# Attention and SwiGLU on one core: first loads from two queues, and the order planned anew

## The chip, the core and the metric

The kernel runs on one core of a Trainium2 chip, as one program. A core has five engines that work beside each other and wait for each other through semaphores: TensorE (PE, matrix products), VectorE (DVE), ScalarE (ACT), GpSimd (POOL) and SyncE (SP, here used only to issue transfers). Transfers between the chip's memory and the core's are issued by an instruction on one engine's queue and carried out by 16 DMA engines. The metric is the device time of one launch in microseconds (us).

## The reference

A forgetting attention over 8 batches of 8 heads, 576 positions and 64 channels, and behind it a feed-forward block with SwiGLU over the 4608 tokens, whose inner width is 1536:

```python
scores = scale * np.matmul(q, k.transpose(0, 1, 3, 2))
cum = np.cumsum(np.log(np.clip(f, 0.0001, 1.0)), axis=-1)
scores = np.where(causal, -1e9, scores + cum[..., :, None] - cum[..., None, :])
attn = np.exp(scores - np.max(scores, axis=-1, keepdims=True))
attn = attn / (np.sum(attn, axis=-1, keepdims=True) + 1e-09)
x = np.matmul(attn, v)          # (8, 8, 576, 64), then (4608, 512)
g = x @ w_gate                  # (512, 1536)
out = (g / (1 + np.exp(-g)) * (x @ w_val)) @ w_out
```

All inputs and the output are float32; the kernel multiplies in bfloat16.

## The kernel before, in words

**Attention** runs over 32 pairs of heads (`p`, four to a batch). A pair's 576 query positions are nine blocks of 64, and the two heads of a pair lie in the two halves of the 128 partitions. Blocks 0 to 3 are part A (`g` = 0) and blocks 4 to 8 part B (`g` = 1). For each pair the steps are:

- loads of `q`, `k` and of the cumulated log gates `cb`, spread over the partitions; the first four pairs get them in parts (`load_parts`, L523), the others whole (`load_pair`, L453 and L460);
- casts to bfloat16 (`qb`, `kb`; L560 to L564, later L481 and L483), transposes on PE (L207) into `tx`, copies out of it into `qz` and `kt` (L589 and L591, later L509 and L511);
- scores on PE into `sp` (L201), with a mask added by a small matmul for the first half of the pairs; DVE adds `cb` and takes the row's minimum at once (L652, tiles `t` and `tm`); ACT takes the exponential and its row sum (L672, tiles `e`, `eo` and `ls`); DVE inverts the sums (`lr`, L688 and L690, or L686 on ACT first); POOL, or ACT for the first eight pairs, multiplies by them (`pk`, L708 or L706);
- `pk` is transposed: for the first eight pairs on PE through `gv` with a copy to `pT` (L743), then by a DMA transpose from SP (L721);
- `pT` times `vt` on PE (L764) and a copy into `xT` (L791), which holds a ring of 2048 tokens, transposed for the feed-forward block.

**The cumulated gates** are made once: `f` is loaded (L398), clipped by DVE (L400), its logarithm taken by ACT (L402), and summed along the positions by a DVE scan (L403). The first pairs get their rows of it by a float32 matmul with a selecting matrix (`select`, L425, copied out at L430); the others read them back from a buffer in the chip's memory (`cum_f`, L412).

**The feed-forward block** runs over twelve tiles of tokens (256, 256, seven of 512, 256, 128, 128). `gate` multiplies `xT` by pieces of `w_gate` and `w_val` (both L201, into `gv`, from `wg` and `wv`), with tanh on ACT (L855) and two products on DVE (L857, L860) into `hh`; `project` multiplies `hh` by `w_out` (`wo`), copies out (L884, L886) and stores (L889). The weights are loaded by POOL, which casts them on the way, in eleven pieces (L824 and L828): `wg2` is columns 256 to 511 of `w_gate`, named after its first block of 128 columns. The first tile of tokens needs part A of all four pairs of the first batch, and for its first group `wg0` and `wv0`, for its second `wg2` and `wv2`.

**What sets the order.** The program names every operation with the engines that could do it and an estimate of its duration on each, with a priority and its dependences. `Plan.order` then places the operations one by one: always the one that could start soonest on some engine (a `bias` can be added to an engine's start for the comparison), ties by priority. That gives each engine's order of instructions, and for operations with a choice also the engine. A buffer is given to its next user in order of priority; `SLACK` (`pl.slack`) says how long one group of users of a pool lets another go first. `NUDGE` shifts the priorities of named groups of operations: `a` a pair's attention part, `q` its preparation, `v` a batch's values, `f` and `o` a tile's gates and projection. No time is measured while the kernel runs; the order is fixed when it is built.

**The line of first loads.** `STARTUP` (L281) lists the first loads in order: `q1` is the last part of pair 1's `q`, `p0` part A of `k` and `q` of pairs 0 and 1 in two halves each (called `k0A` and `q0A` in the prediction), `p2` the same for pairs 2 and 3 (`k2A`, `q2A`), `k0` and `q0` the parts B, `f9` the gates, `c3` the `cb` rows of pair 3, `v04` the fifth block of batch 0's values, `wg2` a piece of weights. The loop at L930 gives them priorities in this order, ties each to the end of the load ten places before it (`AHEAD`), and a load of weights, which is POOL's, to the one six places before (`BEHIND`). These ties hold for the plan. Before the change ACT issues two of the first loads, one half of `k0A` and one of `q0A`, POOL the weights, and SP all others.

Of the kernel before, what the change touches and what calls it, by code (L numbers as in the profile page):

```python
# [214 lines left out]
def kernel(  # L215
# [11 lines left out]
    nc = tc.nc  # L227
# [36 lines left out]


    NHALF = 4
    NSELA = 4
    NSEL = 1
    CUT = QB * (HI[0] + 1)
# [2 lines left out]
    BEHIND = 6  # L272
# [12 lines left out]
    NUDGE = "a0.0:-91 a0.1:-64.5 a1.0:-94.5 a1.1:-57.5 a11.1:-0.5 a12.1:-0.5 a14.0:-1.5 a15.0:-2.5 a16.0:-4 a16.1:-1 a18.0:-0.5 a19.1:-1 a2.0:-83.5 a2.1:-46 a20.0:-0.5 a23.0:-1.5 a24.0:-2.5 a24.1:-1.5 a25.0:-1.5 a25.1:-3 a26.0:0.5 a26.1:-3.5 a28.0:4.5 a29.0:-1 a3.0:-78.5 a3.1:-57 a30.0:3.5 a30.1:0.5 a31.0:22 a31.1:8 a4.0:-42.5 a4.1:-28.5 a5.0:3 a5.1:-39.5 a6.0:-3.5 a6.1:3 a7.0:1.5 a7.1:-13 a8.0:1 a8.1:0.5 f0:-981.5 f11:18.5 f2:3 f4:4 f5:2 f6:-1.5 f8:1 f9:-4 o0:1.5 o1:-18.5 o10:-2 o3:0.5 o5:-5 o6:-1 o7:9.5 o8:-0.5 o9:5 q0:-42.5 q1:-75.5 q11:1 q12:2 q14:-0.5 q15:-0.5 q16:-3.5 q17:-0.5 q18:-6 q20:-5.5 q21:0.5 q22:1.5 q23:1 q24:3.5 q25:2 q28:3 q29:1 q3:1.5 q31:5.5 q5:-0.5 q6:0.5 q8:-1.5 q9:-3.5 v1:-57.5 v2:3.5 v3:5.5 v4:5.5 v5:5.5 v6:2 v7:-2.5"  # L285

    WAIT = ""
    ORDER = [(int(u[0]), int(u[1])) for u in HEAD.split()]
# [7 lines left out]
    pl = Plan()  # L296
# [98 lines left out]
    def gates(key, parts, np_, prio):  # L395
        x = lambda: pl.buf(key)[0:np_, :]
        for n, (a, z, src) in enumerate(parts):
            loads["f", key, n] = pl.op({"SP": 600}, lambda e, a=a, z=z, src=src: nc.sync.dma_start(out=pl.buf(key)[a:z, :], in_=src),  # L398
                                       (), [(key, 0)] + [key] * (n == 0), prio + n * .01, dma=570, pk=93)
        pl.op({"DVE": 760}, lambda e: nc.vector.tensor_scalar(x(), x(), 1.0e-4, 1.0, op0=ALU.max, op1=ALU.min),  # L400
              [(key, 0)], [(key, 1)], prio, holds=[key])
        pl.op({"ACT": 690}, lambda e: nc.scalar.activation(x(), x(), AF.Ln), [(key, 1)], [(key, 2)], prio, holds=[key])  # L402
        pl.op({"DVE": 1350}, lambda e: nc.vector.tensor_tensor_scan(x(), tiny[0:np_, 0:1].to_broadcast((np_, S)), x(), 0.0, ALU.mult, ALU.add),  # L403
              [(key, 2), "tiny"], [(key, 3)], prio, holds=[key])
# [118 lines left out]
    def load_parts(p):  # L523
        b, hp = divmod(p, NPB)
        pl.key(("cb", p), "cb", p)
        for name, x, a, z, r, n in parts(p):
            fk = (name + "f", p, x)
            pl.key(fk, name + "f")
            m = (z - a) // r

            def load(e, u, fk=fk, src=(k if name == "k" else q), a=a, z=z, r=r, m=m):
                h0 = 2 * (hp + u)
                (nc.scalar if e == "ACT" else nc.sync).dma_start(
                    out=pl.buf(fk)[m * u:m * u + m, :, 0:r * D],
                    in_=src[b, h0:h0 + 2, a:z].rearrange("h (p r) d -> p h (r d)", r=r))
# [262 lines left out]
    def load_v(b):  # L798
        for c in range(5):
# [107 lines left out]
    line = []  # L907
# [97 lines left out]
```

## Time and profile before

| | us |
|---|---|
| median of three runs | 413.37 |
| the three runs | 416.99, 413.37, 410.46 |
| the profiled execution | 410.55 |
| its span, first to last instruction | 408.8 |
| PE, busy | 391.2 |
| DVE, busy | 334.5 |
| ACT, busy | 319.8 |
| POOL, busy | 271.5 |

The three engines beside PE have no idle engine's worth of room either: DVE does the scores' sums and the gates' products, ACT the exponentials and tanh. The table's busy times are those of the whole span, but the span has three stages. Up to about 30 us only attention runs, as no tile of tokens is finished. From there to about 330 us attention and the feed-forward block run beside each other, and the rest is the feed-forward block alone. In a row of the timeline the columns are the start, the duration, the engine, line and operation, the tile written and the tiles read, shapes and types, how many instructions are merged, and in brackets the idle time just before with what ended it. In the rows of PE a duration includes the way through the array, so that durations of neighbours overlap.

### The profile page before, as it was taken

Reading aid. Unit: us, or ns where it says so; the run is one execution under the profiler, and the core shown is the slowest. Engines: PE = TensorE matmul, PEld = TensorE weight load, DVE = VectorE, ACT = ScalarE, POOL = GpSimd, SP = SyncE. Lnnn points to the kernel's source line nnn. Section 1 sums busy time; section 2 is a strip of 40 time slices with the busy share of each in tenths; the row PEclk is TensorE's granted clock in tenths of the full one; section 3 lists DMA queues with packets and bytes.
Section 4 is the critical chain, followed back from the end, with each engine's and each line's share of the span. In section 5 each row is a group of like instructions: output and inputs, shape, how many; then the busy total and the mean of one; then the engine's idle time right before and its main releaser. Section 6 shows DMA issues by size and latency. Waiting matters only on the chain.

```text
span 408.8 us, 15353 instructions
## 1 busy us (share of the span) xinstructions
PE 391.2 (96%) x5848; PEld 266.0 (65%) x5848; DVE 334.5 (82%) x1270; ACT 319.8 (78%) x905; POOL 271.5 (66%) x474
## 2 busy tenths in 40 slices
PE   2978899999999999999999999999999999999996
PEld 1657879887776776665655655565565555577766
DVE  4698999979998789989999998899989943775123
ACT  5898999999999989998978998897889753332222
POOL 8579877989888985898798797967957550000000
PEclk9999999999999999999999999999999999999999
DMA  7999997997999999999999999999975584000211
GB/s 203 239 211 188 230 195 142 188 251 203 193 216 176 248 231 202 225 253 226 208 204 234 219 228 216 238 193 208 220 175 110 107 135 130 2 2 2 102 57 53
DMA packets 144026, 72.16 MB, mean 177 GB/s; under 512 B 117904, under 2 KB 131728, under 8 KB 143952
## 3 DMA queue, kind: packets, MB, share of 16 engines
q1 hardware_dynamic: 137856, 66.21, 75.8%
q0 software_dynamic: 5808, 4.72, 7.9%
q8 instruction: 45, 0.74, 0.8%
q14 instruction: 29, 0.24, 0.2%
q10 hardware_dynamic: 288, 0.26, 0.2%
HBM read 46.65 MB, written 9.58 MB: 138 GB/s over the span
## 4 chain that ended last, share of the span: by engine, by line
PE 85%; ACT 3%; DVE 3%; DMA 3%; POOL 3%; issue 1%; POOLq 0%; DVEq 0%; ACTq 0%
PE gv L201 64%; PE sp L201 9%; PE tx L764 5%; PE tx L207 4%; DMA wv<-in_moe_w_val_dram 2%; PE gv L207 2%; DVE t L652 2%; PE gv L425 1%; DMA qf<-in_q_dram 1%; POOL pk L708 1%; ACT eo L672 1%; ACT e L672 1%; ACT pT L743 1%; DVE th L857 0%; ACT qz L589 0%
## 5 line engine op out<-in xcount | busy, mean ns | idle before, releaser
L652 DVE CUSTOM_DVE_ANT_0 t<-sp,cb 128x512 f32<-128x512 f32 (+7 forms) x272 | 121.3, 464 | 9.0 <-PE sp L201 5.4
L708 POOL TENSOR_SCALAR pk<-e,lr 128x128 bf16<-128x128 f32 (+3 forms) x188 | 100.2, 537 | 30.3 <-DVE lr L690 20.5
L201 PE MATMUL gv<-xT,wv 128*64 128x512 bf16 (+2 forms) x1152 | 112.5, 326 | 1.2 <-DMA wv<-in_moe_w_val_dram 1.2
L201 PE MATMUL gv<-xT,wg 128*64 128x512 bf16 (+2 forms) x1152 | 112.6, 326 | 0.0
L201 PE MATMUL gv<-wo,hh 128*64 128x512 bf16 (+1 forms) x888 | 106.1, 373 | 0.0
L857 DVE SCALAR_TENSOR_TENSOR th<-th,gv 128x512 f32<-128x512 f32 x108 | 73.9, 685 | 28.3 <-ACT th L855 26.9
L672 ACT ACTIVATE e<-t,tm 128x192 f32<-128x192 f32 (+4 forms) x160 | 88.9, 557 | 8.4 <-DVE tm L652 7.6
L855 ACT ACTIVATE th<-gv 128x512 f32<-128x512 f32 x108 | 64.0, 593 | 32.9 <-PE gv L201 32.1
L201 PE MATMUL sp<-kt,qz 128*64 128x64 bf16 (+7 forms) x640 | 76.6, 292 | 3.2 <-DVE tm L652 2.4
L860 DVE TENSOR_TENSOR hh<-th,gv 128x512 bf16<-128x512 f32 x108 | 73.8, 684 | 4.6 <-PE gv L201 1.8
L201 PEld LDWEIGHTS <-wg 128*64 128x64 bf16 x1152 | 59.0, 110 | 27.7
L201 PEld LDWEIGHTS <-wv 128*64 128x64 bf16 x1152 | 58.1, 110 | 28.2 <-DMA wv<-in_moe_w_val_dram 1.4
L672 ACT ACTIVATE eo<-t,tm 128x256 f32<-128x256 f32 (+3 forms) x128 | 71.2, 557 | 5.1 <-DVE tm L652 2.7
L708 POOL TENSOR_SCALAR pk<-eo,lr 128x384 bf16<-128x384 f32 (+2 forms) x127 | 67.7, 533 | 9.8 <-DVE lr L690 4.1
L201 PEld LDWEIGHTS <-hh 128*64 128x64 bf16 x888 | 48.9, 110 | 31.2
L201 PEld LDWEIGHTS <-qz 128*64 128x64 bf16 x640 | 41.0, 112 | 21.2 <-issue 4.8
L652 DVE DVE_READ_ACCUMULATOR2_ANT tm<- 128x1 f32 x432 | 35.8, 83 | 0.0
L884 ACT ACTIVATE ot<-gv 128x512 f32<-128x512 f32 (+1 forms) x31 | 18.0, 581 | 22.2 <-PE gv L201 21.9
L652 DVE CUSTOM_DVE_ANT_0 t<-sp,cm,tm 128x64 f32<-128x64 f32 x128 | 34.4, 278 | 0.9 <-PE sp L201 0.2
L672 ACT ACTIVATION_READ_ACCUMULATOR e<-t,tm 128x1 f32 x160 | 30.6, 191 | 0.0
L764 PE MATMUL tx<-pT,vt 128*64 128x320 bf16 (+4 forms) x448 | 29.2, 262 | 1.4 <-DVE pT L743 0.6
L481 POOL TENSOR_SCALAR qb<-qf 72x1024 bf16<-72x1024 f32 x28 | 29.1, 1040 | 1.2 <-DVE tm L652 0.7
(75 smaller groups left out, 436.1 us busy)
## 6 DMA issues: line engine op xcount, KB each, us to landing
out_dram<-ot SPq DMA_DIRECT2D x35, 256.0 KB
vf<-in_v_dram SPq DMA_DIRECT2D x32, 256.0 KB
cb<-cum_f SPq DMA_DIRECT2D x56, 144.0 KB
kf<-in_k_dram SPq DMA_DIRECT2D x28, 288.0 KB
qf<-in_q_dram SPq DMA_DIRECT2D x28, 288.0 KB
wo<-in_moe_w_out_dram POOLq DMA_DIRECT2D x3, 512.0 KB, 5.9
vf<-in_v_dram SPq DMA_DIRECT2D x8, 128.0 KB
wg<-in_moe_w_gate_dram POOLq DMA_DIRECT2D x2, 512.0 KB, 7.7
```

The source lines that it names most:

```text
L201: nc.tensor.matmul(out[c, :], lhsT[:, c], rhs, **kw)
L207: nc.tensor.transpose(out[c, :], src[:, c], ident)
L425: nc.tensor.matmul(pl.buf(bk)[:, 0:z - a], w, pl.buf("fa")[0:BH, a:z], start=True, stop=True)
L481: eng[e].tensor_scalar(dst, src, -scale, 1.0, op0=ALU.mult, op1=ALU.mult)
L652: nc.vector.tensor_tensor_reduce(out=pl.buf(tk)[:, a:z], in0=pl.buf(sk)[:, o:o + z - a], in1=pl.buf(("cm", p))[:, i, :] if own else pl.buf ...
L672: nc.scalar.activation(pl.buf(ek)[:, :L], pl.buf(tk)[:, :L], AF.Exp, bias=pl.buf(("tm", p, g))[:, 0, i:i + 1], scale=-1.0, accum_out=pl.bu ...
L708: eng[e].tensor_scalar(dst, src, r, 1.0, op0=ALU.mult, op1=ALU.mult)
L764: nc.tensor.matmul(xo[r, 0:QB * n], vt[:, c, 2 * hp + h, :], pT[:, a:a + n, 64 * h:64 * h + 64], start=(c == 0), stop=(c == nch - 1))
L855: pl.op({"ACT": 487}, lambda e, u=u: nc.scalar.activation(pl.buf(("th", t, u)), pl.buf(("wg", t, u)), AF.Tanh, scale=0.5), [("wg", t, u)], ...
L857: pl.op({"DVE": 605}, lambda e, u=u: nc.vector.scalar_tensor_tensor(pl.buf(("th", t, u)), pl.buf(("th", t, u)), 1.0, pl.buf(("wg", t, u)), ...
L860: pl.op({"DVE": 605}, lambda e, u=u: nc.vector.tensor_mul(pl.buf(("hh", t, u)), pl.buf(("th", t, u)), pl.buf(("wv", t, u))), [("u", t, u), ...
L884: nc.scalar.mul(pl.buf(ok)[:, a:z], pl.buf(bk)[:, 0:z - a], 0.5)
```

## The change

The first loads of `f`, of the parts A (and of pair 0's parts B) and of batch 0's values may be issued by SP or by ACT, whichever the plan finds free first; ACT's start counts 300 ns later in that comparison (`TOACT`). The tie of a weight load to an earlier load is made only where there is one six places before; without that test an index below nought would have meant a load at the end of the line. `SLACK` goes from 250 to 400. `STARTUP` and `NUDGE` have new values.

```diff
+    TOACT = 300
...
-    SLACK = 250
+    SLACK = 400
...
-    STARTUP = "q1 p0 f9 c0 wg2 v04 p2 k0 k2 v01 q0 q2 v02 wg0 wv0 c3 c4 q3 v00 c1 c2 wv2 wg4 p4 v03 wv4 p5 wg8 c7 c5 wv8 p6 c6 wo0 v11 v13 p7 v14 v10 v12 wo4 wo8"
+    STARTUP = "q1 p0 f9 wg2 v04 p2 k0 k2 v01 q0 v02 q2 wv0 c3 c4 c0 v00 q3 wg0 c1 wv2 c2 wg4 p4 v03 wv4 p5 wg8 c7 c5 p6 c6 wv8 wo0 v14 v13 p7 v10 v12 v11 wo4 wo8"
...
-            loads["f", key, n] = pl.op({"SP": 600}, lambda e, a=a, z=z, src=src: nc.sync.dma_start(out=pl.buf(key)[a:z, :], in_=src),
+            loads["f", key, n] = pl.op({"SP": 600, "ACT": 720}, lambda e, a=a, z=z, src=src: (nc.scalar if e == "ACT" else nc.sync).dma_start(out=pl.buf(key)[a:z, :], in_=src),
...
-            loads[name, p, x] = [pl.op({"ACT": 720} if p == 0 and x == "A" and u == 0 else {"SP": 620}, lambda e, u=u, load=load: load(e, u),
+            loads[name, p, x] = [pl.op({"SP": 620, "ACT": 720} if p == 0 or x == "A" else {"SP": 620}, lambda e, u=u, load=load: load(e, u),
...
-            loads["v", b, c] = pl.op({"SP": 620}, lambda e, c=c, n=n, fk=fk: nc.sync.dma_start(
+            loads["v", b, c] = pl.op({"SP": 620} if b else {"SP": 620, "ACT": 720}, lambda e, c=c, n=n, fk=fk: (nc.scalar if e == "ACT" else nc.sync).dma_start(
...
     for n, o in enumerate(line):
         o.prio = -100 + n * .1
+        o.bias = {"ACT": TOACT}
         if n >= AHEAD:
             o.after.append(line[n - AHEAD])
         if "POOL" in o.engs:
-            o.after.append(line[n - BEHIND])
+            o.after += line[n - BEHIND:n - BEHIND + 1] if n >= BEHIND else []
```

`NUDGE` is left out here: it holds some hundred small numbers in each version. The lines behind the first edit are one higher in the new version, the last ones two.

In the order of instructions that results, PE has the same matmuls in the same number. The first 24 groups of them stand in the same order; then some change places, and the four copies of part A's result into `xT`, all on DVE before, are one on ACT and three on DVE.

More of the change, by code (lines that the diff above doesn't have):

```diff
@@ L280 @@
     CBACK = 5
-    STARTUP = "q1 p0 f9 c0 wg2 v04 p2 k0 k2 v01 q0 q2 v02 wg0 wv0 c3 c4 q3 v00 c1 c2 wv2 wg4 p4 v03 wv4 p5 wg8 c7 c5 wv8 p6 c6 wo0 v11 v13 p7 v14 v10 v12 wo4 wo8"
+    STARTUP = "q1 p0 f9 wg2 v04 p2 k0 k2 v01 q0 v02 q2 wv0 c3 c4 c0 v00 q3 wg0 c1 wv2 c2 wg4 p4 v03 wv4 p5 wg8 c7 c5 p6 c6 wv8 wo0 v14 v13 p7 v10 v12 v11 wo4 wo8"
     HEAD = "00 10 20 30 11 01 31 21"
-    NUDGE = "a0.0:-91 a0.1:-64.5 a1.0:-94.5 a1.1:-57.5 a11.1:-0.5 a12.1:-0.5 a14.0:-1.5 a15.0:-2.5 a16.0:-4 a16.1:-1 a18.0:-0.5 a19.1:-1 a2.0:-83.5 a2.1:-46 a20.0:-0.5 a23.0:-1.5 a24.0:-2.5 a24.1:-1.5 a25.0:-1.5 a25.1:-3 a26.0:0.5 a26.1:-3.5 a28.0:4.5 a29.0:-1 a3.0:-78.5 a3.1:-57 a30.0:3.5 a30.1:0.5 a31.0:22 a31.1:8 a4.0:-42.5 a4.1:-28.5 a5.0:3 a5.1:-39.5 a6.0:-3.5 a6.1:3 a7.0:1.5 a7.1:-13 a8.0:1 a8.1:0.5 f0:-981.5 f11:18.5 f2:3 f4:4 f5:2 f6:-1.5 f8:1 f9:-4 o0:1.5 o1:-18.5 o10:-2 o3:0.5 o5:-5 o6:-1 o7:9.5 o8:-0.5 o9:5 q0:-42.5 q1:-75.5 q11:1 q12:2 q14:-0.5 q15:-0.5 q16:-3.5 q17:-0.5 q18:-6 q20:-5.5 q21:0.5 q22:1.5 q23:1 q24:3.5 q25:2 q28:3 q29:1 q3:1.5 q31:5.5 q5:-0.5 q6:0.5 q8:-1.5 q9:-3.5 v1:-57.5 v2:3.5 v3:5.5 v4:5.5 v5:5.5 v6:2 v7:-2.5"
+    NUDGE = "a0.0:-88 a0.1:-54 a1.0:-95.5 a1.1:-26 a11.0:0.5 a11.1:0.5 a12.1:0.5 a14.1:1.5 a15.0:-1 a15.1:2 a16.0:-1.5 a16.1:1 a17.0:1 a17.1:1 a18.0:0.5 a18.1:0.5 a19.0:-0.5 a2.0:-79 a2.1:-17 a20.0:-1.5 a20.1:1 a21.1:-1 a22.0:-1 a22.1:-0.5 a23.0:-3 a23.1:-0.5 a24.0:-2.5 a24.1:-1.5 a25.0:1 a25.1:-2.5 a26.0:-0.5 a26.1:-3.5 a27.0:-1.5 a27.1:-1.5 a28.0:1 a28.1:4.5 a29.0:-3.5 a29.1:1 a3.0:-77 a3.1:-22 a30.0:1 a30.1:2 a31.0:7 a31.1:5 a4.0:-8.5 a4.1:-6 a5.0:1 a5.1:-9 a6.0:-3.5 a6.1:2 a7.0:1 a7.1:-5.5 a8.0:1 f0:-1.5 f1:-2 f10:-9 f2:-6 f3:3 f4:8.5 f6:2 f7:3 f8:3 f9:-5 o1:-21 o10:-9.5 o2:3 o3:6.5 o4:-3 o5:-2 o7:-8 o8:-2.5 q0:-34.5 q1:-81 q10:4 q11:3 q12:1 q14:-2 q15:1 q16:-2.5 q17:-0.5 q18:-3.5 q19:3.5 q20:-2.5 q22:1.5 q24:-0.5 q25:3 q26:3 q27:2 q28:3 q3:2.5 q31:7 q4:1 q6:-1.5 q8:-2 q9:-3.5 v0:-15.5 v1:-4 v3:5.5 v4:10 v5:5.5 v6:2 v7:35"
     WAIT = ""
```

## The prediction

> **What bounds the kernel now.** I read the page's first two parts, then busy time by stretches, then TensorE's (PE's) waits in the first 80 us, then the instructions in order of time, and last the chain of waits.
>
> ```profile
> PE 391.2 (96%) x5848; PEld 266.0 (65%) x5848; DVE 334.5 (82%) x1270; ACT 319.8 (78%) x905; POOL 271.5 (66%) x474
> ...
> PE   2978899999999999999999999999999999999996
> ...
> DVE  4698999979998789989999998899989943775123
> ACT  5898999999999989998978998897889753332222
> ...
> PE 85%; ACT 3%; DVE 3%; DMA 3%; POOL 3%; issue 1%; POOLq 0%; DVEq 0%; ACTq 0%
> ```
>
> PE is busy for 96% of the span and in the digits short only at both ends; the last line, the chain of waits by engine, is PE for 85%. How short PE falls, the stretches say; the numbers behind each name are busy us.
>
> ```profile
> 0.00:10.00 10.00, 2.70 (x37) 1.79 (x38) 4.85 (x12) 5.45 (x12) 8.52 (x36) 1.00 0.79 200
> 10.00:20.00 10.00, 9.54 (x89) 6.71 (x87) 6.58 (x29) 8.21 (x28) 5.16 (x11) 1.00 1.03 245
> 20.00:30.00 10.00, 7.90 (x140) 5.71 (x137) 9.24 (x41) 9.28 (x34) 8.58 (x16) 1.00 1.05 210
> 30.00:40.00 10.00, 8.61 (x170) 7.39 (x171) 8.65 (x30) 8.33 (x23) 8.88 (x15) 1.00 1.07 197
> 40.00:50.00 10.00, 8.76 (x225) 7.87 (x221) 9.94 (x35) 9.75 (x26) 8.35 (x13) 1.00 1.05 214
> 50.00:60.00 10.00, 9.26 (x212) 8.27 (x213) 9.46 (x31) 9.87 (x28) 7.71 (x12) 1.00 1.17 207
> 60.00:80.00 20.00, 19.46 (x433) 17.78 (x430) 19.50 (x68) 19.46 (x55) 17.00 (x29) 1.00 0.85 164
> ...
> 200.00:250.00 50.00, 50.00 (x664) 29.23 (x662) 47.88 (x209) 43.95 (x132) 44.96 (x73) 1.00 1.11 219
> ...
> 270.00:290.00 20.00, 19.60 (x238) 11.91 (x234) 19.19 (x85) 17.39 (x52) 15.82 (x26) 1.00 0.95 209
> ...
> 345.00:408.80 63.80, 60.48 (x964) 42.44 (x960) 32.27 (x48) 18.74 (x32) 0.00 (x0) 1.00 0.10 35
> ```
>
> The columns are PE, PE's weight load, DVE, ACT, POOL, the granted clock, the DMA share and GB/s. PE's idle time before 80 us is 7.30 + 0.46 + 2.10 + 1.39 + 1.24 + 0.74 + 0.54 = 13.8 us. The last stretch has 3.3, and the rest of the span's 408.8 - 391.2 = 17.6 us is half a microsecond. From 60 us on PE sets the time; from 20 to 60 us DVE and ACT do: DVE is idle for 0.76 + 1.35 + 0.06 + 0.54 = 2.7 us of the 40, ACT for 0.72 + 1.67 + 0.25 + 0.13 = 2.8. The multiplications are the same in both versions (PE's matmuls are equal in number and sizes in the two instruction orders), so the end can move only by PE's idle time and by how fast attention's first pairs come through DVE and ACT. The waits of the first 80 us:
>
> ```profile
> PE tx L207 <- POOL vt L383: 4.1, 1, 4.1
> PE sp L201 <- DVE tm L652: 2.4, 6, 0.7
> PE tx L207 <- POOL qb L562: 1.5, 1, 1.5
> PE tx L207 <- DVE kb L564: 1.2, 1, 1.2
> PE gv L201 <- DMA wv<-in_moe_w_val_dram: 1.2, 1, 1.2
> ```
>
> The first is the time until the first data is there (the memset named merely ended last).
> **The edits with one answer.** The mended slice changes nothing: the first weight load stands sixth in the line, counted from nought, in both versions (`c0` stands for no load, as pair 0 gets its sums by matmul), so its index minus 6 is 0 and it is tied to the first load as before. Price 0. The larger slack and the new nudges act through the order alone, priced below.
>
> **First loads.** By the instruction order ACT issues five loads instead of two: half of `q0A`, `v04`, half of `k2A`, half of `k0B` and `v02`; SP issues three fewer. Both halves of `k0A` are now SP's, so `f` stands one place later there. The start:
>
> ```profile
> 1.19 0.74 SPq L533 DMA_DIRECT2D kf<-in_k_dram  x1
> 1.98 0.61 SPq L533 DMA_DIRECT2D qf<-in_q_dram  x1
> 2.63 0.60 SPq L398 DMA_DIRECT2D t<-in_f_dram  x1
> ...
> 5.19 0.57 DVE L564 CAST kb<-kf 128x512 bf16<-128x512 f32 x1 [1.23 <-DMA kf<-in_k_dram]
> ...
> 6.26 0.47 DVE L400 TENSOR_SCALAR t<-t 64x576 f32<-64x576 f32 x1 [0.50 <-DMA t<-in_f_dram]
> ...
> 7.02 0.68 ACT L402 ACTIVATE t<-t 64x576 f32<-64x576 f32 x1
> ...
> 7.74 1.37 DVE L403 TENSOR_TENSOR_SCAN t<-tiny,t 64x576 f32<-64x576 f32 x1 [1.01 <-ACT t L402]
> ...
> 7.96 0.64 PE L207 MATMUL tx<-ident,qb 128*64 128x128 bf16 x8 [1.51 <-POOL qb L562]
> ...
> 8.64 1.54 ACT L589 COPY qz<-tx 64x256 bf16<-64x256 bf16 x4 [0.94 <-PE tx L207]
> ...
> 9.06 0.81 PE L201 MATMUL sp<-kt,qz 128*64 128x256 bf16 x2 [0.46 <-ACT qz L589]
> ...
> 10.34 3.78 PE L425 MATMUL gv<-t,one 64*128 64x256 f32 x8
> ```
>
> The second half of `k0A` moves from 1.19 to about 1.98, so its cast from 5.19 to 5.98. ACT now does it, for the same 0.57 or a little more: 6.6, and with 0.64 of transposes 7.2. The cast of `q0A` leaves POOL, where it ended just before 7.96, for DVE: about 0.57, ended near 7.2, so its transposes start at 7.3 instead of 7.96 and the scores at 8.4 instead of 9.06. But the selects (L425) wait for the scan. `f` lands at 6.26 + 0.65 = 6.9 and is clipped by 7.4; the logarithm on ACT now stands behind a copy of `qz` that cannot start before the transposes end, 7.95, and takes 1.54 / 4 = 0.4: 8.4 to 9.1. The scan ends at 9.1 + 1.4 = 10.5, and the selects start at 10.5 instead of 10.34: +0.2. Ends: -0.6, if the scan is in time and the selects follow the scores (1.28 from 9.06 to 10.34, so 8.4 + 1.28 = 9.7); +1.3, if `v04` and half of `k2A`, 256 KB now beside `f`, all go ahead of it (256 KB at 200 GB/s). I take the +0.2, nearest to the rows. Behind the issues on ACT stand its casts and copies; where one is delayed by an issue it is by some 0.6, as in the SP rows, and that lies inside these ends. Loads that SP now reaches sooner feed POOL casts which have time: price 0, cover POOL's 4.8 idle us from 10 to 20.
>
> Here the first stretch's DMA share of 0.79 and the following 1.03 to 1.17 say that transfers, not their issue, fill the queue from 10 us on. The Trainium skill's page "DMA: Bandwidth & Descriptors", section "Issuing engines are not separate DMA queues", says the same as a rule: loads started on several engines share the same DMA engines, and only the starting sequencer's time is saved. By that rule this part is worth nothing; by my rows +0.2.
>
> **Casts moved.** The last part of `q0` is now cast by DVE between score steps, and PE's order puts its transposes ahead of the fifth select. That costs 0 to one cast, 0.57: +0.3.
>
> **Weights and the first gate.** `wv0` now goes before `wg0`, and `wv2` has four POOL operations fewer between it and the scores it waits behind.
>
> ```profile
> 26.86 0.80 POOL L824 DMA_DIRECT2D wv<-in_moe_w_val_dram  x1
> ...
> 30.42 1.07 PE L201 MATMUL gv<-xT,wg 128*64 128x256 bf16 x16
> ...
> 35.16 1.06 PE L201 MATMUL gv<-xT,wv 128*64 128x256 bf16 x16 [1.16 <-DMA wv<-in_moe_w_val_dram]
> ...
> 59.05 1.07 PE L201 MATMUL gv<-xT,wv 128*64 128x256 bf16 x16
> ```
>
> ```profile
> L652 DVE CUSTOM_DVE_ANT_0 t<-sp,cb 128x512 f32<-128x512 f32 (+7 forms) x272 | 121.3, 464 | 9.0 <-PE sp L201 5.4
> ```
>
> `wv2` was issued at 26.86 and landed 8.3 us later, for the matmuls at 35.16. In the new order these come behind two more groups of transposes and scores, and the issue is no later: the 1.16 goes, -1.2. What is late next is `xT`: three of its four first copies now stand on DVE behind four more score steps. Those are 4 x 0.46 = 1.9 us; what else DVE takes on and gives away ahead of it (copies of `qz` and casts against copies of `pT`, casts and a copy of `xT`) nearly cancels, and much of what it takes on lies in the first 10 us, where it is idle for 5.15. So the first gate comes at 31 to 32.3 instead of 30.42. I cost that at 0: the twelve gate groups of the first tile spread from 30.42 to 59.05, PE is idle for 5.5 us from 20 to 60, and both orders have the same multiplications ahead of the twelfth. If the cover is gone it costs the 1.9.
>
> **Work moved between engines.** Up to the eighth pair ACT gives five normalizations to POOL and six copies of `qz` to DVE, and takes three copies of `pT`:
>
> ```profile
> 26.30 0.33 DVE L591 COPY qz<-tx 64x320 bf16<-64x320 bf16 x1
> ...
> 27.39 0.41 ACT L589 COPY qz<-tx 64x320 bf16<-64x320 bf16 x1
> ```
>
> ```profile
> L743 ACT COPY pT<-gv 128x768 bf16<-128x768 bf16 x1 | 0.8, 779 | 0.0
> L706 ACT ACTIVATE pk<-e,lr 128x128 bf16<-128x128 f32 x2 | 0.8, 388 | 0.0
> ```
>
> ACT: -5 x 0.39 at least, -6 x 0.41, +3 x 0.78 is -2.1, and some smaller copies leave it too. DVE gets 6 x 0.33 = 2.0 and gives about as much away in `pT` copies and casts. So ACT gets room and DVE none; it can gain only its waits, at most 2.7. I take a third to a half, -1.0.
>
> **After 60 us** PE has 0.4 idle (270 to 290) and the tail, whose order is the same but for buffer numbers: 0.
>
> Sum: 0.2 + 0.3 - 1.2 - 1.0 = -1.7. On the profiled execution (410.55, span 408.8) that is 408.9; on the median of the three runs (413.37) 411.7. The four executions known have the median (410.55 + 413.37) / 2 = 412.0, on which I put it: **410.3**.
>
> **Rivals.** All from 412.0.
> - *Nothing moves*: the loads were bound by transfers, and what DVE gains waits elsewhere. DMA shares above 1 speak for it, the vanishing 1.16 against it. 412.0.
> - *Late first gate, slower*: the four score steps ahead of `xT` on DVE hold back the first tile, whose copies, tanh and products then meet the second pair's scores on a DVE that is 99% busy from 40 to 50. For: that stretch. Against: PE's idle 5.5. Price 1.9 + 0.5 of the start: 414.4. It decides if the twelfth gate group starts later than 61.
> - *Order stalls PE later, much slower*: every one of the 24 pairs from the ninth on costs PE one wait like the 0.4 at 270 to 290, because DVE, at 47.9 of 50, serves scores after the place PE's order expects: 24 x 0.4 = 9.6, so 421.6. Against it: only one such wait now.
> - *Full overlap, faster*: the room on ACT closes PE's gaps from 20 to 60 altogether: 412.0 - 5.5 = 406.5. For: DVE's waits there; against: DVE's own load does not fall.
>
> **Chances.** Forecast 0.36, nothing 0.20, late gate 0.20, later stalls 0.08, full overlap 0.16. The forecast's ends (-0.6, 0, -1.2, -2.7 and +1.3, +0.6, 0, 0) with the runs' scatter make 407 to 415; taking in the late gate and the full overlap, 405.5 to 417 leaves out the later stalls and the outermost scatter. The runs shown differ by 1.6%, so 2% (8.3 us) is about what a measurement here can tell from no change. Faster by more needs the full overlap and a low execution: 0.07. Slower by more is the later stalls: 0.09. Within: 0.84.
>
> **What would show it.** Right: no wait of PE on `wv`; the selects (L426 there) start between 10 and 11; the first gate at 31 to 32.3; the twelfth near 58; PE idle before 80 us near 12. Wrong: selects after 11.5, the twelfth gate group after 61, or waits of `sp` on DVE that add up to microseconds past 100 us.

## The result, and the profile after

The change made the kernel slower by one per cent. Eleven runs of each:

| | before | after |
|---|---|---|
| median, us | 411.48 | 416.45 |
| lowest to highest, us | 409.64 to 416.99 | 414.57 to 418.48 |
| ratio, 95% interval | | 1.0101 (1.0072 to 1.0129) |
| profiled execution, us (its span) | 410.55 (408.8) | 418.17 (416.4) |

The execution that was profiled is one of the long ones of the new kernel, 1.7 us above its median, so its trace shows 7.6 us where the medians differ by 5.0. Other executions of it had spans down to 412.8.

First the page of the changed kernel: busy time by engine, the busy digits of PE and DVE, the chain of waits by engine.

```profile
PE 393.1 (94%) x5848; PEld 269.3 (65%) x5848; DVE 337.8 (81%) x1287; ACT 311.6 (75%) x882; POOL 273.9 (66%) x480
...
PE   2879879999999999999999999999999999999996
...
DVE  4679879989999899979999999799989962775133
...
PE 72%; DVE 8%; DMA 8%; POOL 5%; ACT 3%; issue 2%; SPq 1%; DVEq 0%; POOLq 0%; ACTq 0%
```

PE has the same 5848 matmuls and is busy for almost the same time, 393.1 against 391.2 us, so most of the loss is idle time of PE. The digit 7 in the sixth slice and the chain, which runs over DVE, DMA and POOL for longer than before, say that something holds PE up early. The stretches, with the columns of the prediction's table, say where:

```profile
0.00:10.00 10.00, 2.26 (x28) 1.42 (x30) 4.81 (x15) 3.68 (x7) 7.11 (x36) 1.00 0.90 186
10.00:20.00 10.00, 8.65 (x78) 6.16 (x78) 6.55 (x28) 6.66 (x25) 3.83 (x8) 1.00 0.74 178
20.00:30.00 10.00, 7.49 (x123) 5.41 (x119) 7.60 (x39) 9.27 (x31) 9.60 (x19) 0.83 1.05 215
30.00:40.00 10.00, 9.05 (x196) 7.82 (x197) 9.62 (x36) 9.44 (x26) 8.90 (x16) 1.00 1.11 231
40.00:50.00 10.00, 8.85 (x197) 7.96 (x192) 9.70 (x29) 9.56 (x24) 9.19 (x14) 1.00 1.06 203
50.00:60.00 10.00, 6.52 (x145) 5.45 (x146) 6.70 (x27) 7.58 (x21) 8.34 (x14) 1.00 1.21 200
60.00:80.00 20.00, 19.94 (x468) 18.56 (x465) 19.34 (x67) 18.52 (x49) 14.91 (x25) 1.00 0.83 158
80.00:200.00 120.00, 119.17 (x1809) 77.16 (x1806) 110.56 (x427) 105.94 (x318) 101.33 (x172) 1.00 1.06 214
200.00:250.00 50.00, 49.42 (x634) 31.10 (x632) 47.00 (x208) 43.08 (x129) 40.17 (x68) 1.00 1.13 216
250.00:270.00 20.00, 19.13 (x276) 11.56 (x274) 17.24 (x83) 17.00 (x46) 16.17 (x23) 1.00 1.11 190
...
290.00:345.00 55.00, 54.58 (x658) 33.87 (x656) 46.43 (x204) 41.22 (x123) 36.69 (x63) 1.00 0.88 161
345.00:416.40 71.40, 68.10 (x1042) 49.68 (x1038) 33.48 (x50) 21.41 (x37) 0.00 (x0) 1.00 0.14 47
```

Before 80 us PE is idle for 17.2 us instead of 13.8. The largest piece is 50 to 60 us, 3.48 idle instead of 0.74, and there DVE and ACT have idle time too (6.70 and 7.58 busy, 9.46 and 9.87 before), so none of the three is the bound in that stretch: they wait for each other and, as follows, for a load of weights. From 80 to 345 us PE is idle for 0.83 + 0.58 + 0.87 + 0.42 = 2.7, against 0.55 before; the tail's 3.3 is the same. PE's waits of the first 80 us, in us in all, times and longest:

```profile
PE tx L207 <- POOL qb L563: 6.7, 2, 5.7
PE sp L201 <- DVE tm L653: 2.7, 6, 1.0
PE gv L201 <- DMA wv<-in_moe_w_val_dram: 1.4, 1, 1.4
PE gv L426 <- DVE t L404: 1.0, 1, 1.0
PE gv L207 <- POOL pk L709: 1.0, 2, 0.6
```

In the first row the longest wait, 5.7 us, is the time until PE's first transposes; it was 4.1 before. Before, ACT cast the last part of pair 1's `q` for them; now POOL does, behind its issue of the first weight load. Two rows of the kernel before:

```profile
3.42 0.63 ACT L560 ACTIVATE qb<-qf 80x512 bf16<-80x512 f32 x1 [0.44 <-DMA qf<-in_q_dram]
...
4.10 0.48 PE L207 MATMUL tx<-ident,qb 80*64 80x80 bf16 x8 [4.10 <-POOL vt L383]
```

Three more waits are new: the selects wait for the scan of `f`, PE waits twice for normalizations on POOL, and a wait on `wv` is there again. Rows of the changed kernel in order of time, from the start, then the first gate group and the one that waits:

```profile
3.28 0.63 SPq L399 DMA_DIRECT2D t<-in_f_dram  x1
...
4.00 0.97 POOL L825 DMA_DIRECT2D wg<-in_moe_w_gate_dram  x1
5.05 0.61 POOL L563 TENSOR_SCALAR qb<-qf 80x512 bf16<-80x512 f32 x1
...
5.72 0.48 PE L207 MATMUL tx<-ident,qb 80*64 80x80 bf16 x8 [5.72 <-POOL qb L563]
...
6.46 0.63 ACT L561 ACTIVATE kb<-kf 128x512 bf16<-128x512 f32 x1 [4.23 <-DMA kf<-in_k_dram]
...
8.51 0.45 DVE L401 TENSOR_SCALAR t<-t 64x576 f32<-64x576 f32 x1 [0.17 <-DMA t<-in_f_dram]
...
9.35 0.68 ACT L403 ACTIVATE t<-t 64x576 f32<-64x576 f32 x1
...
10.42 1.35 DVE L404 TENSOR_TENSOR_SCAN t<-tiny,t 64x576 f32<-64x576 f32 x1
...
11.83 3.78 PE L426 MATMUL gv<-t,one 64*128 64x256 f32 x8 [1.05 <-DVE t L404]
...
33.93 1.23 PE L201 MATMUL gv<-xT,wg 128*64 128x256 bf16 x16
...
58.62 1.06 PE L201 MATMUL gv<-xT,wv 128*64 128x256 bf16 x16 [1.40 <-DMA wv<-in_moe_w_val_dram]
```

The selects start at 11.83, right behind the scan and that wait of 1.0; before they started at 10.34, 1.2 us after the scan had ended. The first gate group comes 3.5 us later than before, the twelfth at 62.94 instead of 59.05. The weights that PE waits for at 58.62 are `wv8`, issued by POOL at 45.61; the chain that ended last runs from 33 to 45 us mostly over POOL's normalizations, casts and issues, and then over this load.

How far one kernel is behind another can be read better than from single rows. Both do the same multiplications, so I added up the columns of PE's matmuls in order of their start, and for a given share of that work took the difference of the two times. In us behind the kernel before, each by its profiled execution (labels are those of the experiments below):

| before is at | 24 | 32 | 46 | 52 | 58 | 80 | 120 | 189 | 249 | 309 | 389 |
|---|---|---|---|---|---|---|---|---|---|---|---|
| after | 2.3 | 2.9 | 0.9 | 1.5 | 3.9 | 4.6 | 4.2 | 4.4 | 5.9 | 7.6 | 7.6 |
| e1 | 1.9 | 2.8 | 1.2 | 1.3 | 2.3 | 2.9 | 2.6 | 3.7 | 4.2 | 3.6 | 3.6 |
| e2 | 2.0 | 2.6 | 1.4 | 2.0 | 2.8 | 3.3 | 2.8 | 3.5 | 3.9 | 4.1 | 4.0 |
| e5 | -0.4 | 1.2 | 0.6 | 0.6 | 0.6 | 1.1 | 0.9 | 1.3 | 1.3 | 1.3 | 1.3 |
| x1 | -0.2 | -0.2 | 1.0 | 1.0 | 1.0 | 2.1 | 2.1 | 2.3 | 2.8 | 2.5 | 2.5 |
| x4 | -0.2 | 0.7 | -1.1 | 0.3 | 1.0 | 1.1 | 1.1 | 2.0 | 2.5 | 2.2 | 2.2 |
| y1 | 1.1 | 1.8 | -0.1 | 0.5 | 3.0 | 3.0 | 2.9 | 3.1 | 3.6 | 4.3 | 4.3 |
| z3 | 1.0 | 5.1 | 3.7 | 3.7 | 3.7 | 3.7 | 3.8 | 4.1 | 4.1 | 4.1 | 4.1 |

The new kernel is 3 us late when the first gate is due, has made up 2 of them at 46, loses 3 us between 46 and 58, and in this execution 3 more behind 189. e1 and e2 have the same order behind 62 us, and there they lose nothing and 0.5 behind 189, so the last 3 us seem to belong to the execution that was profiled. The kernel before has a span of 408.8 in its profile and a median of 410.3 in 119 later executions, so some 1.5 us in the later columns of each row is scatter.

### The profile page after: what moved, and what is told of

Its sections match the earlier page's. It is cut to its first block, busy times and chain, and to the rows that moved or that the text cites. A ratio compares the mean times of both kernels' runs of the same rounds, so it can differ in the third digit from the quotient of the medians.

```text
span 416.4 us, 15382 instructions
## 1 busy us (share of the span) xinstructions
PE 393.1 (94%) x5848; PEld 269.3 (65%) x5848; DVE 337.8 (81%) x1287; ACT 311.6 (75%) x882; POOL 273.9 (66%) x480
## 4 chain that ended last, share of the span: by engine, by line
PE 72%; DVE 8%; DMA 8%; POOL 5%; ACT 3%; issue 2%; SPq 1%; DVEq 0%; POOLq 0%; ACTq 0%
PE gv L201 56%; PE sp L201 7%; PE tx L765 4%; POOL pk L709 3%; DMA wv<-in_moe_w_val_dram 3%; DVE t L653 3%; DMA qf<-in_q_dram 3%; PE tx L207 3%; DMA pT<-pk 2%; DVE th L858 1%; PE gv L207 1%; PE gv L426 1%; DVE hh L861 1%; ACT e L673 1%; POOL qb L482 1%
## 5 line engine op out<-in xcount | busy, mean ns | idle before, releaser
L709 POOL TENSOR_SCALAR pk<-e,lr 128x512 bf16<-128x512 f32 (+2 forms) x192 | 101.5, 533 | 31.3 <-DVE tm L653 21.6
L673 ACT ACTIVATE e<-t,tm 128x448 f32<-128x448 f32 (+4 forms) x160 | 88.7, 556 | 7.1 <-DVE tm L653 6.5
L201 PEld LDWEIGHTS <-wv 128*64 128x64 bf16 x1152 | 60.3, 110 | 28.4 <-DMA wv<-in_moe_w_val_dram 1.6
L201 PEld LDWEIGHTS <-wg 128*64 128x64 bf16 x1152 | 60.6, 110 | 27.3 <-issue 0.2
L709 POOL TENSOR_SCALAR pk<-eo,lr 128x128 bf16<-128x128 f32 (+3 forms) x128 | 68.6, 536 | 11.6 <-DVE lr L691 5.6
L201 PEld LDWEIGHTS <-hh 128*64 128x64 bf16 x888 | 50.7, 110 | 29.8
```

The source lines that it names most:

```text
L201: nc.tensor.matmul(out[c, :], lhsT[:, c], rhs, **kw)
L673: nc.scalar.activation(pl.buf(ek)[:, :L], pl.buf(tk)[:, :L], AF.Exp, bias=pl.buf(("tm", p, g))[:, 0, i:i + 1], scale=-1.0, accum_out=pl.bu ...
L709: eng[e].tensor_scalar(dst, src, r, 1.0, op0=ALU.mult, op1=ALU.mult)
```

## The experiments

All were run in alternation with the kernel before, whose medians in these sets were 411.6 to 412.6 us.

| | ratio to before, 95% interval | median, us |
|---|---|---|
| e1, loads issued as before | 1.0074 (1.0043 to 1.0106) | 415.16 |
| e2, `wv8` earlier | 1.0094 (1.0060 to 1.0128) | 416.31 |
| e3, both | 1.0086 (1.0055 to 1.0117) | 416.03 |
| e4, kernel before with the new split of loads | 1.0004 (0.9978 to 1.0030) | 412.44 |
| e5, kernel before with a late gate | 1.0012 (0.9977 to 1.0047) | 412.23 |
| y3, kernel before with more for POOL | 0.9997 (0.9972 to 1.0021) | 412.20 |
| e6, first gate's inputs earlier | 1.0131 (1.0100 to 1.0163) | 417.72 |
| e7, e3 and e6 together | 1.0096 (1.0064 to 1.0127) | 416.09 |
| r1, code alone | 1.0334 (1.0293 to 1.0375) | 425.10 |

**The loads and one weight load.** In e1 to e3 the changed kernel's planned order stands, and only loads are moved in it. In e4 the kernel before issues its first loads from the engines that the changed kernel uses.

```diff
+    seq = pl.order()
+    k0, q0, k2 = loads["k", 0, "A"], loads["q", 0, "A"], loads["k", 2, "A"]
...
+    head = loads["q", 1, "B"] + k0 + q0 + [loads["f", "fa", 0], loads["v", 0, 4]] + k2
+    for o in head + kb + [v2]:
+        o.eng = "SP"
+    k0[0].eng = q0[0].eng = "ACT"
...
+    late = loads["wv", 8]
+    seq.remove(late)
+    seq.insert(seq.index(loads["wg", 8]) + 1, late)
...
```

> The changed kernel with its order kept in all else, but the first loads issued as before the change: SP issues v04, both halves of k2A and of k0B and v02 again, ACT one half each of k0A and q0A ahead of its table load. Theory A (v04 and half of k2A, moved ahead on ACT's queue, share the DMA engines with f, k0A and q0A and delay them): f is clipped near 6.5 to 7 us instead of 8.51, the selects start at 10.3 to 10.7 instead of 11.83, and the whole shortens by 1.2 to 1.6 us, to about 415.0 on the median scale of 416.45 (ratio to before 1.007 to 1.011). Theory B (what is late is w_val's last piece, whose landing does not hang on the start): the selects come earlier and the end does not move, 416.5. Theory C (the issue place alone, not the sharing): f lands 0.65 earlier, 7.9, and no more.

> The changed kernel with its order kept in all else, but the load of w_val's last piece (wv8) issued right after w_gate's (wg8) on POOL, about 41.4 us instead of 45.6. Theory B: the wait of 1.4 us at 58.6 goes, the tenth gate group starts near 55 to 57 instead of 58.62 and the twelfth near 61 instead of 62.94; the whole shortens by 1.5 to 3 us, to about 414. Theory A: the late start holds all behind it anyway, DVE and ACT are the bound and the end moves by less than 0.5 us, 416. Theory D (the DMA queue is full, so an earlier weight delays the loads that it passes): other waits take its place, 416 to 418.

> Both edits together. Theories A and B both right and additive: 416.45 - 1.4 - 2 = about 413, ratio to before near 1.003. If the two share their cause (one late chain), no better than the better of the two alone. Whatever is left over 411.5 belongs to the rest of the new order (casts and copies moved between engines, waits after 80 us, which were 2.3 us longer in the profiles).

> The kernel before with its order kept in all else, but its first loads split as after the change: SP issues both halves of k0A, one of q0A, f and half of k2A; ACT, behind its table load, the other half of q0A, v04 and the other half of k2A. Theory A: f, k0A and q0A land 1 to 2 us later, the selects start near 11.8 instead of 10.34 and the whole grows by 1.2 to 1.6 us, to about 413 (ratio 1.003 to 1.004). Rival: the split is harmless and it was the new order around it: 411.5.

The loads bring 0.3%, with intervals that overlap, and in the kernel before they cost nothing that can be measured. `wv8` brings nothing that can be measured: its ratio differs from the changed kernel's by less than 0.1%, with intervals of 0.3% to either side. So neither is shown to be the main cause. Two limits: in e4 the clipping of `f` was 1.5 us later than before (7.79), but the selects only 0.3 (10.61), so that run does not repeat the late selects. And e3 has a new wait of 1.17 us, on a piece of `w_gate`, ahead of the fifth gate group at 41.90.

The start of e1, DVE's rows and then PE's, shows why giving the loads back is not enough:

```profile
6.25 0.66 DVE L592 COPY qz<-tx 64x320 bf16<-64x320 bf16 x2 [2.27 <-PE tx L207]
6.93 0.75 DVE L563 TENSOR_SCALAR qb<-qf 128x512 bf16<-128x512 f32 x1
7.60 0.85 DVE L401 TENSOR_SCALAR t<-t 64x576 f32<-64x576 f32 x1
8.81 0.92 DVE L592 COPY qz<-tx 64x256 bf16<-64x256 bf16 x3 [0.36 <-ACT qz L590]
9.76 1.35 DVE L404 TENSOR_TENSOR_SCAN t<-tiny,t 64x576 f32<-64x576 f32 x1
```

```profile
11.17 2.07 PE L426 MATMUL gv<-t,one 64*128 64x256 f32 x4 [1.05 <-DVE t L404]
```

The clipping of `f` waits for no transfer here. It stands behind two copies of `qz` and a cast that ACT and POOL did before, and starts at 7.60 instead of 6.26; the scan stands behind three more copies and starts at 9.76 instead of 7.74. The selects are then 0.83 late. The copies could not start earlier, as the first transposes wait for POOL's cast until 5.72 here too. Work that was moved, not the transfer, holds the scan in e1. In e2, with the loads split, the same rows are:

```profile
7.68 0.78 DVE L401 TENSOR_SCALAR t<-t 64x576 f32<-64x576 f32 x1
```

```profile
11.18 2.07 PE L426 MATMUL gv<-t,one 64*128 64x256 f32 x4 [1.05 <-DVE t L404]
```

Here `f` is issued at 3.28 as in the changed kernel, the clipping waits for no transfer either (the cast ahead of it waits 0.30 us for `q`), and the selects start within 0.01 us of those of e1. Of the traces that begin with the changed kernel's first 70 steps, all have the first transposes at 5.72 to 5.74. Their selects start at 11.16 to 11.17 with the loads given back (e1, e3, e7) and at 11.18 to 11.84 without (e2, e6, x2, x3, y2, z2 and the changed kernel). Those that begin with the kernel before's first 70 steps (x1, x4, y1, z1 and z3) have them at 3.88 to 4.14 and at 10.35 to 10.42.

**A late gate and a fuller POOL, in the kernel before.** Its order is kept, and one suspected cost is added to it.

```diff
...
+    move(op("DVE", ("x", 3, 0)), op("DVE", ("t", 1, 5)))
+    move(op("PE", ("wg", 0, 0)), op("PE", ("sp", 3, 1, 0)))
+    move(op("PE", ("wv", 0, 0)), op("PE", ("wg", 0, 0)))
...
```

```diff
...
+    wv0 = op("POOL", ("wv", 0))
+    for o in reversed([o for o in seq if ("pk", 0, 0) in o.writes][2:]):
+        move(o, wv0, "POOL")
...
```

> The kernel before, its own order kept, with one thing moved: the copy of pair 3's first weighted values (x of pair 3, part A) goes four score steps later on DVE, and the first two gate groups (wg, wv of group 0) go behind the first score bank of pair 3's second part; the three small steps that read them move with them. Late-gate theory (a first gate that starts late is lost to the end, since nothing later takes it up): first gate at 32.5 to 33.5 instead of 30.4, twelfth gate group 1.5 to 2.5 later than 59.05, time 1.2 to 2.5 us above before. Cover theory (PE idles 3 to 4 us between 40 and 60 and takes the delay up there): twelfth gate group within 0.5 of 59.05, time within 0.6 of before.

> The kernel before, its own order kept, with the two normalizations of pair 0 that ACT does at 20.5 to 21.2 us given to POOL behind the issue of wv0. POOL then has 0.74 us more (two of 0.37) ahead of the casts of kb, vt and qb. If POOL is the bound from 17 to 30 us: first gate 0.5 to 0.9 later, time 0.4 to 0.9 us above before, ratio 1.001 to 1.002. If POOL has room there: first gate within 0.2 and ratio within 0.001 of 1.

Here is the first gate group and the twelfth of e5:

```profile
32.42 1.06 PE L201 MATMUL gv<-xT,wg 128*64 128x256 bf16 x16
...
59.66 1.07 PE L201 MATMUL gv<-xT,wv 128*64 128x256 bf16 x16
```

The first gate is 2.0 us later than before, the twelfth group 0.6, and the time is the same within 0.5%. That interval alone would leave room for 1.9 us; the trace speaks against a delay that lasts: PE's gaps between 30 and 60 us take most of it up, in that order of steps. In y3 the first gate comes 1.1 us later, at 31.50, and the twelfth group 1.0, at 60.02, with a ratio of 0.9997, whose interval ends 0.9 us above the kernel before. So two more normalizations ahead of POOL's casts cost at most that, in the kernel before. What POOL's load costs in the changed order no run tests.

**The first gate's inputs earlier, in the changed kernel.** Eleven steps that lead to the first gate, and its first two groups, were moved forward, and the cast of the first value tile changed places with a weight issue.

```diff
...
+    move(op("POOL", ("vt", 0), ("vf", 0, 0)), op("POOL", ("pk", 2, 0), n=-1))
+    move(op("POOL", ("wv", 2)), op("POOL", ("pk", 3, 0), n=-1))
+    move(op("ACT", ("pT", 2, 0)), op("DVE", ("t", 0, 7)), "DVE")
+    move(op("PE", ("xo", 1, 0)), op("PE", ("sp", 0, 1, 3)))
...
+    move(op("PE", ("wg", 0, 0)), op("PE", ("sp", 1, 1, 3)))
...
```

> The changed kernel, its order kept but for the first gate's inputs: the cast of the first value tile goes ahead of one weight issue on POOL (they change places over four normalizations), the copies of pT for pairs 2 and 3 and of x for pair 0 go from ACT to DVE, the four weighted products and their copies stand four to eight score steps earlier, and the first two gate groups one bank earlier each. Late-gate theory: first gate at 31.3 to 32.3 instead of 33.9, twelfth gate group 1.0 to 2.0 earlier than 62.9, time 1.0 to 2.0 us under the changed kernel (ratio to before 1.005 to 1.0075). Cover theory (the loss of the changed kernel comes from steps after 62 us, from DVE or POOL there): twelfth gate may be earlier, time within 0.5 of the changed kernel, ratio 1.009 to 1.011.

> The changed kernel with the early gate inputs, with the first loads issued as before, and with wv8 issued next to wg8. If the three losses found so far add (first gate 1.5, start and wv8 together 1.1 of which 0.4 to 1.2 showed): first gate at 30.6 to 31.6, twelfth gate group at 59.0 to 60.5, time 0 to 1.5 us above before, ratio 1.000 to 1.004. If the early part is no bound: ratio stays at 1.007 to 1.010, as with loads and wv8 alone.

In both, the copy of pair 0's part A stands behind pair 2's product in the same buffer, so these tokens take pair 2's values; the amount of work is unchanged. The edit missed its aim: PE waited for the copies of `pT`, now on DVE, and the first gate stayed at 33.89 in e6. It tells only that steps moved by hand bring waits of their own.

**The code alone.** The changed kernel with `SLACK`, `STARTUP` and `NUDGE` of the kernel before.

> The changed kernel's code (engines of the first loads free to the plan, first weights no longer tied) with the start-up list, the slack and the nudges of the kernel before, and the order planned from that. If the three planning inputs carry the loss: first gate at 30 to 31.5, ratio to before 0.996 to 1.003. If the freed engines or the untied weights carry it: first gate at 32 or later, or a PE wait on a weight tile before 62 us, ratio 1.005 or more. An order planned anew can also land anywhere between, by chance of ties; the milestones then say which.

The three new inputs do not carry the loss. With the old ones the same code is 3.3% slower than before, and its order is a different one again: PE waits 3.7 us for a `wv` before 60 us and is idle for 4.38 us from 30 to 40. The new inputs take back 2.3% of that and not the rest. Where small numbers are fitted to one order, they say little about another.

**Exchanging beginnings.** The plan of either kernel has the same 2844 steps. Here the first so many are placed as one kernel places them, on its engines and in its buffers, and the rest follow in the order of the other.

```diff
...
+            if self.first:
+                for i, (n, e, *at) in enumerate(self.first):
+                    o = self.ops[n]
+                    if any(d.start is None for k in o.reads for d in writers[k] if d is not o):
+                        continue
...
+                del self.first[i]
...
```

> Of the 2844 planned steps the first 480 (planned to about 62 us) in the order and on the engines of the kernel before, all others in the order and on the engines of the changed kernel. The two orders have 477 of these 480 steps in common, so the cut is at the same work. If the loss is made before 62 us: ratio to before 1.000 to 1.003. If it is made after 62 us: 1.007 to 1.012. From the traces so far, by the work that PE has done (2.8 of 3.9 us of lag are there at 58 us where loads and wv8 are as before): 1.002 to 1.004.

> The reverse: the first 480 steps as in the changed kernel, all others as in the kernel before. If the loss is made before 62 us: ratio 1.007 to 1.010, with the first gate near 33.9 and the twelfth gate group near 62.9. If after 62 us: 1.000 to 1.003.

> The first 200 steps (planned to about 26 us; 194 of them in common) as in the changed kernel, all others as in the kernel before. This has the late selects, the moved casts and the full POOL queue, and then the order of the kernel before. If what is late in the first 26 us is kept to the end: first gate near 32 to 33, time 1.3 to 2.0 us above before, ratio 1.003 to 1.005. If the idle of PE at 30 to 60 us takes it up, as it took up the late gate: within 0.6 us, ratio 0.9985 to 1.0015.

> The first 200 steps as in the kernel before, all others as in the changed kernel. If the first 26 us carry the loss: ratio 1.003 to 1.006, selects at 10.3. If steps 200 to 480 carry it (the late first value tile, the four weighted products in a row, wv8 behind p6 and c6): ratio 1.006 to 1.010, and PE waits for wv8 at 56 to 59 as in the changed kernel.

> The first 70 steps (the same 70 in both kernels, planned to 11.8 us: first loads, first casts and turns, the sigmoid, log and scan of f, the first scores) in the order and on the engines of the kernel before, all others as in the changed kernel. The first 200 steps as before brought the ratio from 1.010 to 1.0038. If the first 70 carry that (late scan, late selects): ratio 1.003 to 1.006, selects near 10.4. If steps 70 to 200 carry it (POOL: five more normalizations, weight issues between them, the value tile cast late): ratio 1.0075 to 1.010.

> The reverse: the first 70 steps as in the changed kernel, all others as in the kernel before. The first 200 steps of the changed kernel in this place gave 1.0115. If the first 70 carry it: selects at 11.2 to 11.8 and the order behind them runs 0.8 to 1.5 us late to the end, ratio 1.002 to 1.004, or more if the delay grows. If it is taken up before 60 us: ratio 0.999 to 1.0015, and steps 70 to 200 carry the rest.

> The first 140 steps (planned to 19.9 us, 137 in common) as in the kernel before, all others as in the changed kernel. With 70 steps the ratio was 1.0065, with 200 it was 1.0038. If steps 70 to 140 (the first scores, the casts of the second halves) carry the difference: 1.003 to 1.005. If steps 140 to 200 (normalizations on POOL, pT on ACT, the late first value tile) carry it: 1.006 to 1.0075.

> The reverse: the first 140 steps as in the changed kernel, all others as in the kernel before. With 70 steps the ratio was 1.0027, with 200 it was 1.0115. If steps 70 to 140 carry the growth: 1.008 to 1.012. If steps 140 to 200 carry it (their weighted products find no value tile yet): 1.002 to 1.005.

> Only steps 70 to 200 in the order and on the engines of the changed kernel; the first 70 and all behind 200 as in the kernel before. If the loss of the changed kernel's first 200 steps (1.0115) is the sum of its parts, 1.0027 for the first 70, this gives 1.007 to 1.010. If the late start is what makes steps 70 to 200 dear: 1.000 to 1.004.

| first steps | as before, the rest as after | as after, the rest as before |
|---|---|---|
| none | 1.0101 (1.0072 to 1.0129) | 1 |
| 70 | y1: 1.0065 (1.0037 to 1.0093) | y2: 1.0027 (1.0000 to 1.0054) |
| 140 | z1: 1.0072 (1.0036 to 1.0107) | z2: 1.0103 (1.0071 to 1.0135) |
| 200 | x4: 1.0038 (1.0015 to 1.0062) | x3: 1.0115 (1.0086 to 1.0143) |
| 480 | x1: 1.0042 (1.0018 to 1.0066) | x2: 1.0247 (1.0216 to 1.0279) |

z3, which has only steps 70 to 200 from the changed kernel, gives 1.0100 (1.0055 to 1.0146).

In the left column, with the beginning of the kernel before, the changed order loses less: 0.4% less for the first 70 steps, 0.6% for the first 200, nothing more for the next 280. Only the 0.6% is clear of the intervals; the rows of 70 and 140 steps overlap with those beside them, and the 140 stand above the 70. The last 0.4% stays: x1 has the kernel before's beginning to about 62 us and is 2 us slower all the same. The two stretches behind that point in x1 show a part of it:

```profile
60.00:80.00 20.00, 19.25 (x423) 17.97 (x419) 18.89 (x67) 18.74 (x53) 15.91 (x26) 1.00 0.88 171
80.00:100.00 20.00, 19.56 (x390) 15.37 (x387) 17.78 (x71) 18.71 (x56) 18.25 (x34) 1.00 0.96 216
```

PE is idle for 0.75 + 0.44 us, against 0.54 + 0.12 before. By the table of delays 1.0 of x1's 2.5 us is there at 46, over the same steps (PE waits 2.33 us for `wv2` there, 1.16 before), 1.1 comes between 58 and 80, where the two orders are joined, and 0.4 later. So the seam may have a large part in x1's loss.

The right column cannot be read as a sum. 1.0027 and 1.0100 would do for the 1.0115, but the same first 200 steps cost nothing like that before their own continuation, and x2 with 1.0247 is worse than either parent. The traces show what happens there. In x2 a cast of values behind the seam waits 5.39 us for its load, and PE waits 3.81 us for the normalization behind that cast. In z2 PE waits for a weight load whose issue has moved (from 26.86 to 29.17), and in z3 its order, made for a beginning in which the first two weighted products were long done, meets them too early. Two rows of x2, one of z2, then three of z3:

```profile
78.68 1.16 POOL L983 CAST vt<-vf 128x512 bf16<-128x512 f32 x2 [5.39 <-DMA vf<-in_v_dram]
...
80.46 0.32 PE L378 MATMUL gv<-ident,pk 128*64 128x128 bf16 x2 [3.81 <-POOL pk L880]
```

```profile
39.09 1.57 PE L369 MATMUL gv<-xT,wv 128*64 128x256 bf16 x16 [2.63 <-DMA wv<-in_moe_w_val_dram]
```

```profile
28.28 0.53 PE L932 MATMUL tx<-pT,vt 128*64 128x256 bf16 x4 [0.68 <-POOL vt L979]
29.40 0.53 PE L932 MATMUL tx<-pT,vt 128*64 128x256 bf16 x4 [0.59 <-DVE xT L959]
30.91 0.53 PE L932 MATMUL tx<-pT,vt 128*64 128x256 bf16 x4 [0.98 <-DVE pT L911]
```

In z3 the delay stands at 5.1 us when the kernel before is at 32 and is still 3.8 at 120. The changed kernel has the same late value tile, but its own PE order does scores first there, and its delay falls from 2.9 to 0.9 by 46 us. By these traces a late start is cheap or dear by what the order behind it expects.

## Why the prediction was wrong

The time, 416.45, lies inside the range and the sign is wrong: I forecast 1.7 us gained, and 5.0 were lost by the medians, 4.2 by the ratio. By the steps of the prediction:

- **First loads, +0.2 (ends -0.6 and +1.3): this step failed, in its mechanism.** The selects were put at 10.5 and came at 11.83 here and at 11.18 in e2, which has the same first loads. The sum followed `f`'s transfer and had PE's first transposes and DVE as before. It had not seen that the cast for those transposes goes from ACT to POOL, behind the issue of a weight load (5.72 instead of 4.10), nor that copies and a cast would stand ahead of the clipping and the scan on DVE. In e2 these alone make the selects 0.84 late. The split loads add up to 0.7 us to that, and in some traces nothing: here DVE waits 0.67 us for `q` and 0.17 for `f`, which was expected at 6.9 and clipped at 8.51; in e2 it waits 0.30 and nothing. So that the selects came near the +1.3, whose reason was 256 KB ahead of `f`, is in the main chance. The end is dearer by some 1.1 to 1.5 us for the first 70 steps (y2: 1.0027; y1: 0.0036 less than the changed kernel), with intervals that reach nought. By the rule of the Trainium skill's page "DMA: Bandwidth & Descriptors", section "Issuing engines are not separate DMA queues", the split was worth nothing; e4 (1.0004) agrees.
- **Casts moved, +0.3: as forecast.** From the first select to the fifth it is 5.39 us (11.83 to 17.22) instead of 5.13 (10.34 to 15.47).
- **Weights, -1.2: half right.** The wait on `wv2` went, as forecast. A wait of 1.40 on `wv8` took its place; `STARTUP` now names `wv8` behind `p6` and `c6`, which I had not followed, and it was issued 1.7 us later than before. In e1 it was issued at 45.66 and PE did not wait for it, so the landing differs between executions too. And neither wait is worth what it shows: without the one on `wv8`, e2 and e3 gained nothing that can be measured, so a wait counted in full as a gain was an error even where it went.
- **The late first gate, cost 0: not contradicted, though its marks were passed.** The first gate came at 33.93, later than the 31 to 32.3 forecast, and the twelfth group at 62.94, later than the 61 from which the rival was to decide. Its mechanism is not shown to be the cause: e5 and y3 delay the gate by 2.0 and 1.1 us and are not measurably slower, and the changed kernel itself is only 0.9 us behind at 46. The mark could not tell the late gate from the later stall.
- **Work moved between engines, -1.0: this step failed.** It credited the room on ACT. By the stretches to 60 us, DVE was busy for 45.0 us instead of 48.7 and ACT for 46.2 instead of 50.9, of which only 2.1 had been moved away. Neither engine got through its work sooner; both waited, for late selects at first and in the stretch from 50 to 60, where PE, DVE and ACT all wait. This is read from the stretches; no run takes the moves back one by one. The price of the same step at the other end, work of DVE ahead of the scan, was left out. POOL's five more normalizations had no price in the sum; POOL is busy for 9.60 of 10 us from 20 to 30, and y3 puts a price only on two of them, in the other order.
- **After 60 us, 0: probably too low.** I had compared the tail and not the whole. x1, equal to the kernel before up to there, is 0.42% slower (0.18 to 0.66), some 1.7 us, with no single wait of PE of more than 0.4 us behind it; the seam may be part of that. The rival of 24 stalls did not come.

In place of -1.7 the runs thus show 2.6 us from the first 200 steps (0.63%, give or take 0.37), of which some 1.5 fall to the first 70 and some 1.1 to the others, neither clear of nought by itself. Another 1.6 to 1.7 come from behind step 480, the seam included, in the order in which the left column takes them away. Two things stay open. One is which of the steps 70 to 200 cost, since the two directions of exchange disagree: z1 puts it behind 140, z2 ahead of it. The other is what makes the order behind 62 us slower, if it is not the seam.

## What to carry to other kernels

Where several engines wait for each other in turn, a wait in the table is not a price: taking it away (`wv8`) or adding one (a late gate, a fuller POOL) may change nothing that can be measured, so ask what the order would do with the time before crediting it. Follow the chain that feeds the first bulk of work through every engine's new order, since a cast ahead of the first transposes or of the scan holds up everything behind it. Read the same row in several traces before naming its cause: the wait for `f`'s transfer was in one trace and the late selects were in all. Numbers fitted to one plan are part of that plan: a code change that makes the order come out anew must be judged as a whole, and parts of two good orders joined together can be worse than either.

## What the runs showed of the hardware that was not expected

Four windows of the changed kernel's trace, with the granted clock as the last column but two:

```profile
24.00:26.00 2.00, 1.04 (x26) 0.73 (x26) 1.99 (x12) 1.78 (x10) 1.96 (x4) 0.91 1.32 217
26.00:28.00 2.00, 1.63 (x26) 1.16 (x22) 1.90 (x10) 1.85 (x6) 2.00 (x5) 0.50 1.24 242
```

```profile
22.22:25.63 3.41, 1.71 (x45) 1.33 (x46) 2.74 (x19) 3.19 (x14) 3.33 (x7) 1.00 1.07 196
...
55.69:59.10 3.41, 1.00 (x19) 0.62 (x15) 2.19 (x9) 3.24 (x9) 3.19 (x6) 1.00 1.27 202
```

The clock fell to half; with means of 0.91, 0.50 and 0.74 from 24 to 30 us, that makes some 3.4 us at half, from about 25.6 on. Ahead of the fall PE was busy for 1.71 of 3.41 us. From 55.69 on it was busy for only 1.00 of 3.41, and the clock stayed full, so the busy share alone does not decide it. The Trainium skill's page "TensorE: Matmul & The Clock Gate", section "Part 1: The HAM clock gate", tells of such a half rate when PE has not been busy for a window of about 3.4 us; the half rate agrees, but here no gap of PE between 20 and 26 us was longer than 1 us. The profile of the kernel before has no such fall inside its span, and its mean clock was 0.996 or less in 20 of 119 executions; their median span is 412.3 against 410.1 us for the others. Of the changed kernel's eleven executions five had such a mean. It is not the cause of the loss, as e1 to e3 are slow at the full clock too, and it goes with only a part of the scatter: the others of the kernel before still have spans from 407.9 to 414.2.

The other surprise is how much the arrival of one early transfer can differ. With `v04` and half of `k2A`, 256 KB, from the second queue beside it and an issue at 3.28 instead of 2.63, the clipping of `f` waited for it until 8.51 here (6.26 before) and until 7.79 in e4, and did not wait at all in e2, where it started at 7.68.
